# A gated attention + Fourier-mixing kernel: operands of the next sequence product at an even rate, reciprocals fifteen steps behind their load, x blocks a cycle sooner

## The chip, the cores and the metric

One core of a Trainium2 chip. The metric is device time in microseconds (us) of one execution, the median over repeated runs; lower is better.

## The reference, cut to what matters

```python
g = sigmoid((A_x * gate_w).sum(-1, keepdims=True))      # A_x: 1 x 2048 x 640
q, k, v = split(A_x @ wqkv)                             # 32 heads of 20
o = softmax(q @ k.T * 20 ** -0.5) @ v
a = o @ wo
hr, hi = B_x @ dft_hid_re.T, B_x @ dft_hid_im.T         # 640 x 640 each
b = dft_seq_re @ hr - dft_seq_im @ hi                   # 2048 x 2048 each
out = g * a + (1 - g) * b
```

All is float32. The output is 2048 x 640.

## The kernel before, in words

**Precision and products.** TensorE multiplies in a rounded float32 form. Each operand is therefore split into a rounded part and its remainder (`split`: a CAST, L130 on POOL, and a subtraction, L131), and a product is three matmuls. Both Fourier products are done on halves by a scheme with seven products in place of eight: `FEATURE` lists those along the hidden axis, `PRODUCTS` those along the sequence. Each names the sum or difference of one or two blocks that makes its left operand, its right operand, and the one or two targets it is added to.

**The stages.** First the projections, up to about 230 us (queries, keys, values; spilled to DRAM as `qk_scr`, `v_scr`). Then one long loop of 256 cycles, in which attention is interleaved with fill work. Last a tail that applies `wo` to the final rows.

**The cycle.** An attention unit is one head pair and half of the queries; there are 32 (`NU`), each of 32 steps, and a cycle is four steps. In a cycle TensorE does 8 score matmuls for the exponentials (L1071, "e" in the string `ORDER`), 8 score matmuls for the row maxima of a unit that comes 43 steps later (L191, "m"), a share of the fill matmuls ("F"), and at its end ("B", `burst`) the 16 value matmuls of two key tiles (L716, into `av`). ACT takes the exponentials (L1077), DVE reduces the maxima (L193). Score matmuls share five PSUM banks `ps`: one can start when ACT or DVE has read the bank's last contents.

**The fill.** For 56 cycles (`HID`) it is the hidden product (L500): seven features of 8 cycles. A feature has a left operand `lefts` (made of x blocks loaded from `in_xh` into stage tiles and summed and split on POOL: `load_left`, a list of functions of which one runs per cycle) and two right sets (`load_right`, tile `wb`, loaded in two halves from `w_scr`, each set for 4 cycles). The result is read by ACT and DVE into a `raw` tile (L509, L510), added to its targets on POOL (L513) and spilled to `a_scr`. Then come 168 cycles of the sequence product (L797): seven products of 8 tiles, each tile 3 cycles and 16 `dft_step`s. Its operands are `c` (a Fourier matrix, loaded from `in_cdft`, summed in L658 or, the first two, L677, and split into `part`; one for each 8 dft steps) and 16 `a` tiles per product (loaded from `a_scr` as `araw` by `load_a`, L686, summed in L691 and split). Results are added to earlier ones in `finish_y` (L895) and spilled. The `a` tiles of a product are made while the product before it runs. Last come 30 half tiles of the output projection.

**Who queues what.** Every engine takes its instructions in the order of the program. Nearly all transfers are issued by one queue, SP: an instruction there that waits (for data to be written, for a buffer to come free, or for an earlier transfer's landing) holds all transfers behind it. `at_step(i, fn)` puts a function's instructions at step i, whichever engines they go to.

**The end of a unit** (`unit_end`). ACT copies `av` to `o`; the row of sums goes to DRAM (`store_l`, L730) and comes back over 128 partitions (`load_l`, L733, tile `lc`); DVE takes the reciprocal (`recip`, L736); that goes out and comes back as a broadcast (`store_r`, L739, `load_r`, L743, tile `rb`); POOL multiplies (`norm`, L746); `store_o` (L754) writes `o_scr`. These seven stand at the steps in the tuple `steps`. The row maxima of a unit are turned in `turn_max`, whose result goes through DRAM too (L234, L240), in every unit.

**Calls that the change touches.** `run_extras` runs once a cycle: it issues at most one `load_a` and finishes at most one. `load_c_first` loads the first two `c` of the sequence product while the hidden stage still runs; the function that it returns does the POOL work.

Of the kernel before, what the change touches and what calls it, by code (L numbers as in the profile page):

```python
# [83 lines left out]
def f32(ap):  # L84
    return ap.bitcast(F32)
# [3 lines left out]
def mix_kernel(ctx: ExitStack, tc: tile.TileContext, xa, xh, wqk, wb, wr, cdft, wo, out):  # L89
# [61 lines left out]
    def raw_tile():  # L151
        return work.tile([P, 1024], F32, name="raw", bufs=3)
# [24 lines left out]
    def at_step(i, fn):  # L177
        later.setdefault(i, []).append(fn)
# [251 lines left out]
    def load_left(n, stage):  # L430
        terms = FEATURE[n][0]
        hi, lo = [block(z, 2 + n % 2) for z in range(2)]

        def load(q):
            c = slice(1024 * q, min(1024 * q + 1024, ND * 512))
            raws = stage(q)[:, : len(terms), : c.stop - c.start]
            at = sorted(2 * th + dh for _, th, dh in terms)
            sp.dma_start(raws, xh[at[0] : at[-1] + 1 : max(at[-1] - at[0], 1), :, c].rearrange("t p c -> p t c"))
            return raws

        def slab(j, raws):
            c = slice(512 * j, 512 * j + 512)
            parts = [raws[:, z, j % 2 * 512 : j % 2 * 512 + 512] for z in range(len(terms))]
            a = parts[0]
            if len(terms) > 1:
                one, two = parts if terms[0][1:] < terms[1][1:] else parts[::-1]
                pool.tensor_tensor(a, one, two, op=ALU.add if terms[1][0] > 0 else ALU.subtract)  # L447
            split(hi[:, c], lo[:, c], a, pool, pool)

        lefts[n] = [l.rearrange("p (d c) -> p d c", d=ND) for l in (hi, lo)]  # L450
        raws = {}

        def step_(j):
            def fn():
                if j < 2:
                    raws[j] = load(j)
                if j:
                    slab(j - 1, raws[(j - 1) // 2])
                if j == 2:
                    raws[2] = load(2)  # L460
            return fn

        return [step_(j) for j in range(ND + 1)]

    def own_stage(q):
        return f32(stages[q % 2])
# [193 lines left out]

        return finish

    c_raws = []

    def load_c_first(g):
        if g == 0:
            w = f32(wide.tile([P, 2, ND, BW], R, name="wb", bufs=2)).rearrange("p z d c -> p (z d c)")
            c_raws.extend(w[:, 1024 * q : 1024 * q + 1024] for q in range(3))
        (_, th, ri), (sign, th2, ri2) = PRODUCTS[0][0]
        raws = [c_raws.pop(0) if c_raws else raw_tile() for _ in range(2)]  # L670
        for raw, (half, part) in zip(raws, ((th, ri), (th2, ri2))):
            o = (2 * part + g % 2) * 1024
            sp.dma_start(raw, cdft[half * HT + g // 2, :, o : o + 1024])

        def finish():
            c = cparts[g] = part_tile()
            pool.tensor_tensor(raws[0], raws[0], raws[1], op=ALU.add if sign > 0 else ALU.subtract)  # L677
            split(c[:, 0], c[:, 1], raws[0], pool, pool)

        return finish  # L680
# [40 lines left out]
    def unit_end(i, n):  # L721
        o = pa.tile([P, 512], F32, name="o", bufs=2)
        act.activation(o, av, AF.Copy)
        lc = pa.tile([P, 16], F32, name="lc")
        rb = pa.tile([P, 512], F32, name="rb")

        q = pool if n == NU - 1 else sp

        def store_l():
            q.dma_start(l_scr[n], o.rearrange("(j r) c -> j r c", j=4)[:, DH])  # L730

        def load_l():
            q.dma_start(lc, l_scr[n].rearrange("j (a b) -> (j a) b", b=16))  # L733

        def recip():
            dve.reciprocal(lc, lc)  # L736

        def store_r():
            q.dma_start(r_scr[n].rearrange("j (a b) -> (j a) b", b=16), lc)  # L739

        def load_r():
            for j in range(4):
                q.dma_start(rb[32 * j : 32 * j + 32, :], r_scr[n, j : j + 1].to_broadcast([32, 512]))  # L743

        def norm():
            pool.tensor_tensor(o, o, rb, op=ALU.mult)  # L746

        def store_o():
            for qc in range(2):
                for h in range(2):  # L750
                    j = 2 * qc + h
                    t0 = (n % 2) * (S // 2) + qc * 512
                    r = (2 * (n // 2) + h) * DH
                    q.dma_start(o_scr[r : r + DH, t0 : t0 + 512], o[32 * j : 32 * j + DH, :])  # L754

        if n == NU - 1:
            chain.extend((o, rb))
            return
        steps = (6, 10, 18, 25, 29, 36, 46) if n < NU - 2 else (1, 4, 10, 12, 15, 19, 21)
        for k, fn in zip(steps, (store_l, load_l, recip, store_r, load_r, norm, store_o)):  # L760
            at_step(i + k, fn)

# [11 lines left out]
    def dft_step(g):  # L774
        n, t, s = g // NS // HT, g // NS % HT, g % NS
        if s == 0:
            new_y(0), new_y(1)
            outs[n, t] = []
        if s % 8 == 0 and g // 8 + 3 < 2 * UNITS:
            cfin.append(load_c(g // 8 + 3))  # L780
        if s % 8 == 4 and cfin and 2 < g // 8 + 2 < 2 * UNITS:
            cfin.pop(0)()
        if s == 8:
            for _, th, hf in PRODUCTS[n][2]:
                tt = th * HT + t
                y = None
                if (tt, hf) in signs:
                    y = apool[0].tile([P, HE], F32, name="yt", bufs=4)
                    sp.dma_start(y, y_scr[tt, :, hf * HE : (hf + 1) * HE])
                outs[n, t].append(y)  # L790
        c = cparts[g // 8]
        cs = slice((s % 8) * P, (s % 8 + 1) * P)
        a = at[n % 2, s]
        for z, (cz, az) in enumerate(((0, 0), (0, 1), (1, 0))):
            for h in range(2):
                r = slice(64 * h, 64 * h + 64)
                pe.matmul(yp[h][:, :HE], c[r, cz, cs], a[r, az], start=s == 0 and z == 0, stop=s == NS - 1 and z == 2)  # L797
            if z < 2:
                yield
        w = g % (HT * NS) - 16  # L800
        if n + 1 == len(PRODUCTS) and w >= 0:
            d, r = divmod(w, 8)
            if r == 0 and d < ND:
                wos[d] = raw_tile()[:, :D]
                sp.dma_start(wos[d], wo[:, d])
            if r == 5 and d < ND:
                raw = wos.pop(d)
                for h in range(2):
                    wos[d, h] = a_tile(1, 2 * d + h)
                    split(wos[d, h][:, 0], wos[d, h][:, 1], raw[:, h * HE : (h + 1) * HE], pool, pool)  # L810
        if s == NS - 1:
            m = apool[0].tile([P, HE], F32, name="m", bufs=2)
            y0, y1 = yp[0][:, :HE], yp[1][:, :HE]

            def read():
                act.activation(m, y0, AF.Copy)
                dve.tensor_tensor(m, y1, m, op=ALU.add)

            extras.append((now[0], read))
            for out_, y in zip(PRODUCTS[n][2], outs.pop((n, t))):  # L820
                extras.append((now[0] + 5, functools.partial(finish_y, out_, t, m, y)))
        yield
# [33 lines left out]
    def out_tile(tt, hf):  # L856
# [7 lines left out]
        for d in range(ND - 1):  # L864
            for z, (oz, wz) in enumerate(((0, 0), (0, 1), (1, 0))):
# [5 lines left out]
        m = apool[0].tile([P, HE], F32, name="m", bufs=2)  # L871
        y0, y1 = yp[0][:, :HE], yp[1][:, :HE]
        g = gate[:, tt : tt + 1]

# [33 lines left out]
    def run_extras(g, most):  # L908
        while extras and most and extras[0][0] <= now[0]:
            extras.pop(0)[1]()  # L910
            most -= 1
        if more(g):
            n = g // (HT * NS) + 1
            preps.append(load_a(n, made.setdefault(n, 0)))
            made[n] += 1
        if len(preps) > 2 or preps and not more(g):
            preps.pop(0)()

    def more(g):
        n, w = divmod(g, HT * NS)  # L920
        return n + 1 < len(PRODUCTS) and w >= 16 and made.get(n + 1, 0) < NS

    apool = []

# [93 lines left out]
    def end(i):  # L1018
        if i % 4 == 2:
            c = i // 4  # L1020
            n, k = divmod(c, 8)
            if c < HID:
                if c % 4 == 0 and 2 <= c // 4 + 1 < SETS:
                    for q, fn in enumerate(load_right(c // 4 + 1)):
                        at_step(i + 1 + 4 * q, fn)
                if k == 0 and n + 1 < len(FEATURE):
                    slabs.extend(load_left(n + 1, own_stage))
                if slabs:
# [5 lines left out]
                    at_step(i + 2, make_a_early)  # L1034
                if HID - 8 <= c < HID - 2:
                    at_step(i + 4, make_a_early)
                if c in (HID - 4, HID - 2):
                    at_step(i + 5, load_c_first((c - HID + 4) // 2))
            if c == HID:
                make_a_early()  # L1040
                make_a_early()
# [90 lines left out]
    def out_half(tt, hf, y, ops, add, shared=False):  # L1132
# [4 lines left out]
        ye = y[:, hf * HE : (hf + 1) * HE]  # L1137
        g = gate[:, tt : tt + 1]
        if shared:
            m = apool[0].tile([P, HE], F32, name="m", bufs=2)  # L1140
# [99 lines left out]
```

## Time and profile before

| | before |
|---|---|
| median of 3 runs | 1878.33 us (1878.31 to 1878.79) |
| the profiled execution's own time | 1871.42 us |
| its span | 1869.6 us |
| TensorE busy | 1844.7 us, 99% |
| DVE / POOL / ACT busy | 78% / 70% / 66% |

The profiled execution was 6.9 us shorter than the median of the runs without a profile; its span is the part of it between the first and the last instruction. TensorE's busy time is modelled at the ends of its matmuls, so 99% does not say that it works at its best rate. L numbers are lines of the kernel before; in the one after, lines behind the function `load_c_first` are lower by 4.

### The profile page before, as it was taken

How to read it: one execution, taken by the hardware profiler on the slowest of the kernel's cores; microseconds unless marked ns; L12 is line 12 of the kernel's file. 1: busy time of each engine (PE TensorE's matmuls, PEld its weight loads, DVE VectorE, ACT ScalarE, POOL GpSimd, SP SyncE). 2: the span in 40 equal slices, each digit the busy share in tenths (PEclk: the TensorE clock that was granted, in tenths of full speed). 3: DMA queues.
4: the chain of work that ended last, by engine and by line, in shares of the span. 5: the costliest groups of instructions: out<-in, count | busy, mean ns of one | idle time of the engine just before them, and what ended most of it. 6: DMA issues, size and time to landing. Idle time of an engine off the chain costs nothing. (4 is left out here: it accounts for less than half of the span.)

```text
span 1869.6 us, 45887 instructions
## 1 busy us (share of the span) xinstructions
PE 1844.7 (99%) x17917; PEld 1339.1 (72%) x17917; DVE 1459.2 (78%) x2428; ACT 1236.0 (66%) x2378; POOL 1300.1 (70%) x1098
## 2 busy tenths in 40 slices
PE   9999999999999999999999999899999999999998
PEld 8988876676676677776777767667777677766666
DVE  4157488888888888888888888788888888889953
ACT  4233377677676676676776767567767677677785
POOL 1379635566486998566799899868779988734344
PEclk9999999999999999999999999999999999999999
DMA  7887874887886774536577676546486756542214
GB/s 234 202 267 285 256 225 120 205 229 169 233 209 192 226 215 149 139 116 182 184 210 234 164 238 192 166 131 197 137 231 212 212 175 180 157 103 76 63 54 155
DMA packets 194445, 342.26 MB, mean 183 GB/s; under 512 B 53951, under 2 KB 107327, under 8 KB 193971
## 3 DMA queue, kind: packets, MB, share of 16 engines
q1 hardware_dynamic: 193267, 337.35, 61.7%
q0 software_dynamic: 960, 1.97, 0.6%
q8 instruction: 141, 2.31, 0.5%
q14 instruction: 77, 0.63, 0.1%
HBM read 257.79 MB, written 81.28 MB: 181 GB/s over the span
## 5 line engine op out<-in xcount | busy, mean ns | idle before, releaser
L193 DVE TENSOR_REDUCE mx<-ps 128x1 f32<-128x512 f32 x2048 | 1299.4, 685 | 211.4 <-PE ps L191 192.1
L1077 ACT ACTIVATE p<-ps 128x512 f32<-128x512 f32 x2048 | 1087.3, 598 | 440.0 <-PE ps L191 229.9
L191 PE MATMUL ps<-kst,qst 60*128 60x512 f32 x2048 | 778.7, 414 | 11.1 <-DVE mx L193 10.8
L1071 PE MATMUL ps<-qst,kst 62*128 62x512 f32 x2048 | 695.8, 414 | 0.0
L797 PE MATMUL yp<-x,part 64*128 64x320 f32 x5376 | 644.3, 306 | 0.0
L797 PEld LDWEIGHTS yp<-x,part 64*128 64x128 f32 x5376 | 582.3, 186 | 7.2
L716 PE MATMUL av<-p,v 128*21 128x512 f32 x4096 | 495.3, 599 | 0.0
L1071 PEld LDWEIGHTS ps<-qst,kst 62*128 62x128 f32 x2048 | 333.3, 185 | 223.0 <-DVE mx L193 131.5
L191 PEld LDWEIGHTS ps<-kst,qst 60*128 60x128 f32 x2048 | 368.2, 184 | 23.6 <-DVE mx L193 11.9
L131 POOL TENSOR_TENSOR part<-raw,part 128x1024 fp32r<-128x1024 f32 (+3 forms) x134 | 296.8, 2215 | 10.2
L716 PEld LDWEIGHTS av<-p,v 128*21 128x21 f32 x4096 | 95.6, 100 | 209.5 <-issue 208.5
L130 POOL CAST part<-raw 128x1024 fp32r<-128x1024 f32 (+2 forms) x127 | 125.0, 985 | 135.5 <-PE yp L797 102.3
L500 PE MATMUL yp<-wb,x 64*128 64x320 f32 x1680 | 209.3, 308 | 4.9 <-ACT raw L509 3.3
L658 POOL TENSOR_TENSOR raw<-raw,raw 128x1024 f32<-128x1024 f32 x78 | 188.1, 2412 | 33.2 <-DMA raw<-in_cdft 21.4
L500 PEld LDWEIGHTS yp<-wb,x 64*128 64x128 f32 x1680 | 180.8, 186 | 8.9 <-ACT raw L509 3.9
L131 POOL TENSOR_TENSOR x<-araw,x 128x320 fp32r<-128x320 f32 x96 | 83.8, 873 | 7.7
L868 PE MATMUL yp<-x,part 64*128 64x320 f32 x720 | 87.3, 309 | 0.0
L513 POOL TENSOR_TENSOR x<-x,raw 128x640 f32<-128x640 f32 x40 | 62.5, 1562 | 29.9 <-DVE raw L510 17.8
L885 POOL TENSOR_TENSOR x<-x,m 128x320 f32<-128x320 f32 x30 | 26.2, 873 | 81.9 <-DVE m L880 66.8
L868 PEld LDWEIGHTS yp<-x,part 64*128 64x128 f32 x720 | 75.4, 185 | 2.7
L691 POOL TENSOR_TENSOR araw<-araw 128x320 f32<-128x320 f32 x80 | 69.9, 874 | 2.9 <-DMA araw<-a_scr 2.9
L447 POOL TENSOR_TENSOR part<-part 128x512 f32<-128x512 f32 x25 | 32.3, 1292 | 46.1 <-PE ps L191 22.8
(107 smaller groups left out, 1394.3 us busy)
## 6 DMA issues: line engine op xcount, KB each, us to landing
raw<-in_cdft SPq DMA_DIRECT2D x189, 512.0 KB
araw<-a_scr SPq DMA_DIRECT2D x176, 160.0 KB
wb<-w_scr SPq DMA_DIRECT2D x28, 800.0 KB
qk_scr<-p SPq DMA_DIRECT2D x40, 512.0 KB
kst<-qk_scr SPq DMA_DIRECT2D x90, 160.0 KB
qst<-qk_scr SPq DMA_DIRECT2D x90, 160.0 KB
part<-in_xh SPq DMA_DIRECT2D x10, 1024.0 KB
yt<-y_scr SPq DMA_DIRECT2D x64, 160.0 KB
```

The lines of the kernel that those rows point to most:

```text
L130: e1.tensor_copy(dst1, src)
L131: e2.tensor_tensor(dst2, src, f32(dst1), op=ALU.subtract)
L191: pe.matmul(ps, q[b : b + KROWS, qt * P : (qt + 1) * P], k[b : b + KROWS, kc * 512 : (kc + 1) * 512], start=True, stop=True)
L193: return lambda: dve.tensor_reduce(mx[n][:, h, qt, kc : kc + 1], ps, axis=AX.X, op=ALU.max)
L500: pe.matmul(ps[z], lefts[n][a][r, d, k * P : k * P + P], rights[2 * n + hf][r, b, d], start=done_ == 0, stop=done_ == 3 * ND - 1)
L658: pool.tensor_tensor(raws[0], raws[0], raws[1], op=ALU.add if PRODUCTS[n][0][1][0] > 0 else ALU.subtract)
L691: pool.tensor_tensor(raws[0], raws[0], raws[1], op=ALU.add if PRODUCTS[n][1][1][0] > 0 else ALU.subtract)
L716: pe.matmul(av[32 * j : 32 * j + DH + 1, :], v[:, kt, h * (DH + 1) : (h + 1) * (DH + 1)], pp[qc][:, h, :], start=kt == 0, stop=kt == NS - 1)
L797: pe.matmul(yp[h][:, :HE], c[r, cz, cs], a[r, az], start=s == 0 and z == 0, stop=s == NS - 1 and z == 2)
L868: pe.matmul(yp[h][:, :HE], o[r, oz, d], wos[d, hf][r, wz], start=d == 0 and z == 0, stop=d == ND - 2 and z == 2)
L1071: pe.matmul(pt, k[b : b + KROWS + 2, kt * P : (kt + 1) * P], q[b : b + KROWS + 2, qc * 512 : (qc + 1) * 512], start=True, stop=True)
L1077: act.activation(pts[n, kt, qc][:, h], pt, AF.Exp, scale=float(DH) ** -0.5)
```

## The change

Six edits, in the same file:

- `load_left`: the sum and split of an x block run two steps of the list after its load, not one, so the list is one longer. The third load comes at the fourth entry, not the third.
- `load_right` calls: the second half of a set is issued 2 steps after the first, not 4.
- `load_c_first`: is called two cycles sooner, for c = HID - 6 and HID - 4; its POOL work stands 9 steps later, not 5. The first pair goes to the block that will hold `a` tiles 12 to 15, the second to the free `wb` tile.
- `unit_end`: new steps.
- the tile `m`: three buffers, not two (in all three places).
- `run_extras`: a `load_a` is issued when 7 more dft steps of the product have gone by (from the 11th on), not in every cycle from the 16th on, and its POOL work is due 8 steps after its load.

```diff
-                if j:
-                    slab(j - 1, raws[(j - 1) // 2])
-                if j == 2:
+                if j > 1:
+                    slab(j - 2, raws[(j - 2) // 2])
+                if j == 3:
                     raws[2] = load(2)
...
-        return [step_(j) for j in range(ND + 1)]
+        return [step_(j) for j in range(ND + 2)]
...
-    c_raws = []
-
     def load_c_first(g):
-        if g == 0:
-            w = f32(wide.tile([P, 2, ND, BW], R, name="wb", bufs=2)).rearrange("p z d c -> p (z d c)")
-            c_raws.extend(w[:, 1024 * q : 1024 * q + 1024] for q in range(3))
+        w = f32(wide.tile([P, 2, ND, BW], R, name="wb", bufs=2)).rearrange("p z d c -> p (z d c)") if g else f32(block(1, 3))
         (_, th, ri), (sign, th2, ri2) = PRODUCTS[0][0]
-        raws = [c_raws.pop(0) if c_raws else raw_tile() for _ in range(2)]
+        raws = [w[:, 1024 * q : 1024 * q + 1024] for q in range(2)]
...
-        steps = (6, 10, 18, 25, 29, 36, 46) if n < NU - 2 else (1, 4, 10, 12, 15, 19, 21)
+        steps = (4, 8, 23, 26, 30, 38, 47) if n < NU - 2 else (1, 4, 10, 12, 15, 19, 21)
         for k, fn in zip(steps, (store_l, load_l, recip, store_r, load_r, norm, store_o)):
             at_step(i + k, fn)
...
-            m = apool[0].tile([P, HE], F32, name="m", bufs=2)
+            m = apool[0].tile([P, HE], F32, name="m", bufs=3)
...
         if more(g):
             n = g // (HT * NS) + 1
-            preps.append(load_a(n, made.setdefault(n, 0)))
+            preps.append((now[0] + 8, load_a(n, made.setdefault(n, 0))))
             made[n] += 1
-        if len(preps) > 2 or preps and not more(g):
-            preps.pop(0)()
+        if preps and preps[0][0] <= now[0]:
+            preps.pop(0)[1]()

     def more(g):
         n, w = divmod(g, HT * NS)
-        return n + 1 < len(PRODUCTS) and w >= 16 and made.get(n + 1, 0) < NS
+        return n + 1 < len(PRODUCTS) and made.get(n + 1, 0) < min(NS, (w - 4) // 7)
...
-                        at_step(i + 1 + 4 * q, fn)
+                        at_step(i + 1 + 2 * q, fn)
...
-                if c in (HID - 4, HID - 2):
-                    at_step(i + 5, load_c_first((c - HID + 4) // 2))
+                if c in (HID - 6, HID - 4):
+                    at_step(i + 9, load_c_first((c - HID + 6) // 2))
```

On SP, in the hidden stage where the second right set of the fifth feature is loaded (`wb` twice: its two halves; `in_xh`: x blocks of the next feature; `kst`: keys of the next head pair), before:

```order
L438 DMA part<-in_xh 128x1024
L1006 DMA kst_92<-qk_scr 20x4x512
L1006 DMA wb<-w_scr 64x2x1600
L1006 DMA kst_92<-qk_scr 20x4x512 x2
L1006 DMA a_scr<-part 128x640
L560 DMA v<-v_scr 128x672
L1006 DMA kst_92<-qk_scr 20x4x512
L730 DMA l_scr<-o 4x512
L438 DMA part<-in_xh 128x1024
L1006 DMA kst_92<-qk_scr 20x4x512
L1006 DMA wb<-w_scr 64x2x1600
```

and now:

```order
L438 DMA part<-in_xh 128x1024
L1002 DMA kst_92<-qk_scr 20x4x512
L1002 DMA wb<-w_scr 64x2x1600
L1002 DMA kst_92<-qk_scr 20x4x512
L726 DMA l_scr<-o 4x512
L1002 DMA kst_92<-qk_scr 20x4x512
L1002 DMA wb<-w_scr 64x2x1600
L1002 DMA a_scr<-part 128x640
L560 DMA v<-v_scr 128x672
L1002 DMA kst_92<-qk_scr 20x4x512
L438 DMA part<-in_xh 128x1024
```

The second half of the set has moved ahead of five transfers, one of them the next x block; the store of the sums, `l_scr`, has moved up too and still stands before it.

On SP, some 20 steps later in the same unit, where the reciprocals go out (`r_scr`) and the turned maxima too (`m_scr`, and back into `qst`), before:

```order
L1006 DMA a_scr<-x_2662 128x640
L1006 DMA wb<-w_scr 64x2x1600
L739 DMA r_scr<-lc 128x16
L234 DMA m_scr<-m 128x64
L1006 DMA a_scr<-x_2662 128x640
L240 DMA qst_93<-m_scr 1x32x32 x4
L743 DMA rb<-r_scr 32x512 x4
```

and now:

```order
L1002 DMA wb<-w_scr 64x2x1600 x2
L1002 DMA a_scr<-x_2662 128x640
L234 DMA m_scr<-m 128x64
L735 DMA r_scr<-lc 128x16
L1002 DMA a_scr<-x_2662 128x640
L240 DMA qst_93<-m_scr 1x32x32 x4
L739 DMA rb<-r_scr 32x512 x4
```

The store of the reciprocals now stands behind that of the maxima.

On POOL, in the last cycles of the hidden stage (the pairs L130 and L131 with `x` make `a` tiles of the first sequence product, L513 adds hidden results, and the three with 128x1024 make the first `c`), before:

```order
L513 TENSOR_TENSOR x_3493<-x_3493,raw 128x640
L130 CAST x_8217<-part 128x320
L131 TENSOR_TENSOR x_8217<-part,x_8217 128x320
L677 TENSOR_TENSOR wb<-wb 128x1024
L130 CAST part<-wb 128x1024
L131 TENSOR_TENSOR part<-wb,part 128x1024
L130 CAST x_8217<-part 128x320
L131 TENSOR_TENSOR x_8217<-part,x_8217 128x320
L513 TENSOR_TENSOR x_3897<-x_3897,raw 128x640
```

and now:

```order
L673 TENSOR_TENSOR x_7960<-x_7960 128x1024
L130 CAST part<-x_7960 128x1024
L131 TENSOR_TENSOR part<-x_7960,part 128x1024
L130 CAST x_8223<-part 128x320
L131 TENSOR_TENSOR x_8223<-part,x_8223 128x320
L513 TENSOR_TENSOR x_3493<-x_3493,raw 128x640
L130 CAST x_8223<-part 128x320
L131 TENSOR_TENSOR x_8223<-part,x_8223 128x320
L130 CAST x_8223<-part 128x320
L131 TENSOR_TENSOR x_8223<-part,x_8223 128x320
L513 TENSOR_TENSOR x_3894<-x_3894,raw 128x640
```

The first `c` has moved ahead of one hidden result and two `a` tiles, about a cycle.

More of the change, by code (lines that the diff above doesn't have):

```diff
@@ L870, in out_tile @@
                     yield
-        m = apool[0].tile([P, HE], F32, name="m", bufs=2)
+        m = apool[0].tile([P, HE], F32, name="m", bufs=3)
         y0, y1 = yp[0][:, :HE], yp[1][:, :HE]
@@ L1139, in out_half @@
         if shared:
-            m = apool[0].tile([P, HE], F32, name="m", bufs=2)
+            m = apool[0].tile([P, HE], F32, name="m", bufs=3)
             act.activation(m, ps, AF.Copy, scale=g)
```

## The prediction

> **What bounds the kernel now.** I read the page's first part, then the spacing of TensorE's work over time, then its waits, then who made them last.
>
> ```profile
> PE 1844.7 (99%) x17917; PEld 1339.1 (72%) x17917; DVE 1459.2 (78%) x2428; ACT 1236.0 (66%) x2378; POOL 1300.1 (70%) x1098
> ```
>
> TensorE is the bound, and the change leaves its matmuls as they are. So only time that it loses can be won. The busy share hides part of that loss, since it can be busy at a lower clock. A better measure is the start of the 16 value matmuls that end each cycle (timeline of PE: start, length, line, count). Two quiet stretches give the normal cycle, five others are too long:
>
> ```profile
> 355.23 0.63 PE L716 MATMUL av<-p,v 128*21 128x512 f32 x4
> 372.30 0.63 PE L716 MATMUL av<-p,v 128*21 128x512 f32 x4
> 460.01 0.63 PE L716 MATMUL av<-p,v 128*21 128x512 f32 x4
> 478.58 1.06 PE L716 MATMUL av<-p,v 128*21 128x512 f32 x8
> 566.25 0.63 PE L716 MATMUL av<-p,v 128*21 128x512 f32 x4
> 573.57 0.63 PE L716 MATMUL av<-p,v 128*21 128x512 f32 x4
> 586.13 1.06 PE L716 MATMUL av<-p,v 128*21 128x512 f32 x8
> 595.40 1.06 PE L716 MATMUL av<-p,v 128*21 128x512 f32 x8
> 1176.08 0.63 PE L716 MATMUL av<-p,v 128*21 128x512 f32 x4
> 1196.40 1.06 PE L716 MATMUL av<-p,v 128*21 128x512 f32 x8
> 1675.95 1.06 PE L716 MATMUL av<-p,v 128*21 128x512 f32 x8
> ```
>
> Hidden stage: 14 cycles from 372.30 to 460.01, 6.265 us each. Sequence stage: 76 cycles from 1196.40 to 1675.95, 6.31 us each. Against these: A, two cycles from 355.23: 17.07 - 12.53 = 4.54 too long. B, two from 460.01: 18.57 - 12.53 = 6.04. C, one from 566.25: 7.32 - 6.265 = 1.05. D, one from 586.13: 9.27 - 6.265 = 3.00. E, two from 1176.08: 20.32 - 12.62 = 7.70. Together 22.3 us, 1.2% of the time, 14.6 of it in the hidden stage. Their causes, in the waits of TensorE and DVE (us in total, times, longest):
>
> ```profile
> PE ps L191 <- DVE mx L193: 10.8, 4, 5.9
> PE yp L500 <- ACT raw L509: 3.3, 2, 2.7
> PE yp L500 <- DMA wb<-w_scr: 1.6, 1, 1.6
> DVE lc L736 <- DMA lc<-l_scr: 12.2, 4, 6.1
> ```
>
> The four PE waits on the row maxima are DVE standing at the reciprocal, because `lc` has not landed; no bank of maxima comes free meanwhile. The timeline has all four, here with the issue of the first and the last load, and TensorE's wait behind the first:
>
> ```profile
> 346.70 0.35 SPq L733 DMA_DIRECT2D lc<-l_scr  x1
> 361.85 0.25 DVE L736 RECIPROCAL lc<-lc 128x16 f32<-128x16 f32 x1 [2.24 <-DMA lc<-l_scr]
> 362.70 0.50 PE L191 MATMUL ps<-kst,qst 60*128 60x512 f32 x1 [1.81 <-DVE mx L193]
> 468.25 0.25 DVE L736 RECIPROCAL lc<-lc 128x16 f32<-128x16 f32 x1 [2.75 <-DMA lc<-l_scr]
> 571.02 0.25 DVE L736 RECIPROCAL lc<-lc 128x16 f32<-128x16 f32 x1 [1.07 <-DMA lc<-l_scr]
> 1176.36 0.33 SPq L733 DMA_DIRECT2D lc<-l_scr  x1
> 1185.89 0.25 DVE L736 RECIPROCAL lc<-lc 128x16 f32<-128x16 f32 x1 [6.11 <-DMA lc<-l_scr]
> ```
>
> So A, B, C and E hold one each. In A stands another short one (the smaller of the two waits on `raw`, 3.3 - 2.7 = 0.6), in B the late `wb` half, and D is the other `raw` wait. The gaps sum to 10.8 + 3.3 + 1.6 = 15.7 us; the other 6.6 are slow matmuls behind them:
>
> ```profile
> 350.00:370.00 20.00, 17.64 (x159) 11.13 (x149) 13.65 (x25) 11.10 (x23) 14.07 (x12) 0.91 0.81 202
> 1180.00:1190.00 10.00, 4.13 (x33) 3.37 (x33) 3.67 (x7) 1.76 (x4) 9.65 (x11) 0.67 0.62 155
> 1200.00:1210.00 10.00, 10.00 (x110) 7.27 (x110) 8.71 (x15) 7.16 (x14) 4.45 (x3) 1.00 0.61 181
> ```
>
> In the first two of these stretches the granted clock (third number from the end) is 0.91 and 0.67; in the last, a quiet one, 1.00. In A the gaps are 0.6 + 1.81 = 2.4 of 4.54 us, so a short wait costs nearly its length again. The Trainium skill ("TensorE: Matmul & The Clock Gate", Part 1) has the clock halve only after an idle window of about 3.4 us; by that, only E would have slow matmuls behind it, and the loss to be won would be 15.7 + (7.70 - 5.9) = 17.5. The trace speaks against it in A.
>
> **The reciprocal.** It moves from step 18 to 23, its load from 10 to 8. A step is 6.27 / 4 = 1.57 us, so DVE comes to it 7.8 us later. Before, DVE came 2.24, 2.75, 1.07 and 6.11 too soon. Even if the loads land no sooner, 5.1 us are spare in the hidden stage and 1.7 in E; the two steps sooner in the queue (up to 3.1 us) come on top. The term is the 10.8 us of gaps with their slow matmuls: of A all but the 0.6, 3.9; of B by its share of the waits, 6.04 x 2.75 / (2.75 + 1.62) = 3.8; C 1.05; E 7.70; some 16.5.
>
> What it could cost: the store of the reciprocals now waits for an instruction 5 steps later, and holds all of SP behind it.
>
> ```profile
> SPq L234 <- DVE m L131: 208.9, 28, 10.7
> SPq L739 <- DVE lc L736: 104.4, 14, 20.6
> ```
>
> But SP already waits 208.9 / 28 = 7.5 us at the store of the turned maxima, for a DVE instruction in a burst behind the new place of the reciprocal. The reciprocals' store now stands behind that one, so it finds its data ready and adds nothing. I take 0; without this cover it would be up to 5 steps, 7.8 us, of late transfers in a unit. `norm` gets 8 steps behind `load_r`, before 7. The store of the sums stands 2 steps sooner, and SP can wait there 3.1 us longer for ACT; behind it stand `kst` loads with 8 steps to spare, and the second `wb` half.
>
> **Second half of a right set.**
>
> ```profile
> 436.96 0.64 SPq L1006 DMA_DIRECT2D wb<-w_scr  x1
> 450.92 0.64 SPq L1006 DMA_DIRECT2D wb<-w_scr  x1
> 464.12 0.38 PE L500 MATMUL yp<-wb,x 64*128 64x320 f32 x1 [1.62 <-DMA wb<-w_scr]
> ```
>
> It took 13.2 us to land and was 1.62 late. It stands 2 steps sooner, and ahead of the x block. That is 3.1 us at least, so the wait goes, worth the rest of B, 6.04 - 3.8 = 2.2. The x block behind it comes some us later, but its sum stands a whole cycle (6.27) later. I put x blocks and the third `m` buffer at 0: no PE wait names either.
>
> **First `c` operands.**
>
> ```profile
> 573.26 0.88 SPq L673 DMA_DIRECT2D wb<-in_cdft  x2
> 581.89 2.40 POOL L677 TENSOR_TENSOR wb<-wb 128x1024 f32<-128x1024 f32 x1 [10.87 <-PE av L716]
> 589.17 1.53 POOL L513 TENSOR_TENSOR x<-x,raw 128x640 f32<-128x640 f32 x1
> 590.73 0.44 ACT L509 ACTIVATE raw<-yp 128x320 f32<-128x320 f32 x1 [3.46 <-POOL x L513]
> ```
>
> POOL stood 10.87 us at the first sum (the releaser named is long done; it ends 8.6 us after the loads' issue), so the hidden result behind it was added late, `raw` stayed taken, and D followed. Now the loads are called two cycles (12.5 us) sooner and the sum only one. The loads have 9 steps (14.1 us), more than 8.6. D goes: 3.00. What is late next on POOL has 10.87 us more room.
>
> **Even rate of the `a` tiles.** On POOL, E's surroundings give the price of one `y` pair, one `a` tile (from its start to the next) and one `c` (sum to the next CAST):
>
> ```profile
> 1180.61 1.68 POOL L895 TENSOR_TENSOR yt<-yt,m 128x320 f32<-128x320 f32 x2
> 1182.24 0.87 POOL L691 TENSOR_TENSOR araw<-araw 128x320 f32<-128x320 f32 x1
> 1184.52 0.86 POOL L691 TENSOR_TENSOR araw<-araw 128x320 f32<-128x320 f32 x1
> 1186.79 2.37 POOL L658 TENSOR_TENSOR raw<-raw,raw 128x1024 f32<-128x1024 f32 x1
> 1192.65 1.06 POOL L130 CAST part<-raw 128x1024 fp32r<-128x1024 f32 x1
> ```
>
> An `a` tile is 2.28, a `c` 5.86. Where both have two terms, a cycle needs 16/24 x 5.86 = 3.91, plus 8/24 x 1.68 = 0.56, plus one `a`: 6.75 against a cycle of 6.31, for 16 cycles. Now it is 16 `a` tiles in some 22 cycles, 1.66: 6.13. POOL stops falling behind by 0.44 us a cycle. TensorE doesn't wait for it today, so I take 0; it helps SP, which waits for these buffers.
>
> **Sum.** 16.5 + 2.2 + 3.0 = 21.7, and the 0.6 in A: the 22.3 us, near enough. For that 0.6 the x block's third load now stands behind a store of `raw` that it stood ahead of. Removing waits exposes others, though: the transfers stay as dense as they are. I leave one new wait of the mean size of the old four, 10.8 / 4 = 2.7. So 19.6 us go: the profiled execution from 1871.42 to 1851.8, the median (6.9 us above it) from 1878.33 to 1858.7.
>
> **Rivals.**
>
> *The waits move (0.20).* In the hidden stage SP is held by transfers' landings, a load of 8 KB took 15.15 us, and sooner transfers only change who is late. For it: A to D hold waits of three kinds. Against it: each late one gets 3 us or more. E goes and half of the hidden stage's loss stays: 1878.33 - 7.70 - 7.3 = 1863.3; with all of it, 1870.6.
>
> *The slow matmuls stay (0.08).* Of the 6.6 us of slow matmuls, 7.70 - 5.9 = 1.8 follow the one long wait. The other 4.8 could have a cause that isn't the short waits ahead of them, and stay: 1858.7 + 4.8 = 1863.5. For it speaks only that the waits and the clock are read from one execution; against it, that the clock is 1.00 in the quiet stretch. By the 3.4 us of the Trainium skill's page above it would be so.
>
> *POOL comes too late for a product's first tile (0.08), slower.* The last `a` tile is now made at the product's end, about 16 dft steps (3 cycles, 18.9 us) ahead of its use; before, by its place in the code, some 6 cycles. POOL was busy 9.65 of 10 us around E. If its lag passes 18.9 us, TensorE waits at each of six product starts. At the price of E, that is 6 x 7.70 = 46.2, less 22.3: 1902. Against it: 6.13 is under 6.31, so the lag shouldn't grow.
>
> *It does nothing (0.04).* The DMA could land later than 15 steps, or fresh waits use the whole gain: 1878.
>
> **Numbers.** The forecast, 1858.7, has 0.60. Low end: all 22.3 go (1856.0), and a part of the 6.9 us that the runs have over the profile is waits of the same kind: 1851. High end: only E goes, 1871. Outside are the slower case, the case of no change and a little more. A measurement tells 0.2%, 3.8 us, from none. Faster by more: 0.60 + 0.20 + 0.08 = 0.88; same 0.04; slower 0.08.
>
> **What would show it.** DVE's waits for `lc` and PE's waits on `mx` behind them are gone, and 1180 to 1190 has no counterpart at a clock of 0.67. No wait on `wb<-w_scr`; POOL's first sum of `c` waits under 2 us. SP's wait at the reciprocals' store shrinks from 104.4, and its wait at the turned maxima doesn't grow by more than that. All cycles of the sequence stage near 6.31. I am wrong if PE waits for `part`, `x` or `wb` that it didn't wait for before, or if the 22.3 us go and the median doesn't follow.

## The result, and the profile after

| | before | after |
|---|---|---|
| median | 1878.32 us (1874.48 to 1878.79) | 1862.75 us (1861.49 to 1863.75) |
| profiled execution, span | 1871.42, 1869.6 us | 1862.77, 1861.0 us |

The kernel got faster: ratio 0.9921, with an interval of 0.9904 to 0.9938. That is 15.6 us; 19.6 were forecast, and 1862.75 lies in the range but next to the rival "the waits move" (1863.3). On a second chip the same pair had 0.9951 (0.9933 to 0.9969), 9.2 us. Before's median there was 1873.05 us over 29 runs, and 1873.95 and 1873.63 on the two other chips used below, so its four runs in the table are some 5 us higher than elsewhere; whether the chip or the draw made them so is not known.

The page's first part shows the same work, TensorE still the bound:

```profile
PE 1843.7 (99%) x17917; PEld 1343.2 (72%) x17917; DVE 1459.7 (78%) x2428; ACT 1236.9 (66%) x2378; POOL 1300.6 (70%) x1098
```

The spacing of the value matmuls after (timeline of PE), at the places where before lost its time:

```profile
461.31 0.63 PE L712 MATMUL av<-p,v 128*21 128x512 f32 x4
472.90 0.63 PE L712 MATMUL av<-p,v 128*21 128x512 f32 x4
567.11 0.63 PE L712 MATMUL av<-p,v 128*21 128x512 f32 x4
581.02 0.63 PE L712 MATMUL av<-p,v 128*21 128x512 f32 x4
1174.93 0.63 PE L712 MATMUL av<-p,v 128*21 128x512 f32 x4
1187.54 0.63 PE L712 MATMUL av<-p,v 128*21 128x512 f32 x4
```

The last two rows bound two cycles: 12.61 us, against 20.32 in E. E is gone. But the first pair bounds one cycle of the hidden stage, 11.59 us long, and the second pair one of 13.91: 5.33 and 7.64 too long. They stand where B and C were. Summed over all cycles, with 6.265 us for a normal one of the hidden stage and 6.31 in the sequence stage, before lost 14.8 us in the hidden stage and 8.0 in the sequence stage; after loses 14.1 and 1.2. (These sums take in small losses too, so they are a little above the 14.6 and 7.70 of the prediction.) Of the 8.6 us between the two spans, 0.7 come from the hidden stage.

What took the old waits' place stands in the waits of TensorE, and in the timeline of PE with the two waits:

```profile
PE ps L191 <- DMA qst<-qk_scr: 4.8, 1, 4.8
PE ps L191 <- DMA o_scr<-o: 3.8, 2, 3.5
467.10 0.76 PE L191 MATMUL ps<-kst,qst 60*128 60x512 f32 x1 [3.45 <-DMA o_scr<-o]
574.30 0.76 PE L191 MATMUL ps<-kst,qst 60*128 60x512 f32 x1 [4.85 <-DMA qst<-qk_scr]
```

No wait on `mx`, `wb` or `raw` is left. Both new ones are at L191, the first row-maximum matmul of a head pair, which needs that pair's keys and queries. The first row names a store as releaser, but L191 doesn't read that; SP's timeline shows the last query loads just ahead:

```profile
456.33 4.26 SPq L1002 DMA_DIRECT2D qst<-qk_scr  x4
462.37 3.02 SPq L750 DMA_DIRECT2D o_scr<-o  x4
```

The fourth was issued by 460.6 and TensorE went on at 467.10, at least 6.5 us later. I take its landing for what ended the wait. The same two places before:

```profile
461.30 4.21 SPq L1006 DMA_DIRECT2D qst<-qk_scr  x3
474.19 0.50 PE L191 MATMUL ps<-kst,qst 60*128 60x512 f32 x1
```

There the last one was issued by 465.5, and TensorE, held up in B by other waits, came 8.7 us later and found it landed. The old waits had covered the queries.

### The profile page after: what moved, and what is told of

It is laid out like the page before. It is cut to its first block, busy times and chain, and to the rows that moved or that the text cites. A ratio compares the mean times of both kernels' runs of the same rounds, so it can differ in the third digit from the quotient of the medians.

```text
span 1861.0 us, 45882 instructions
## 1 busy us (share of the span) xinstructions
PE 1843.7 (99%) x17917; PEld 1343.2 (72%) x17917; DVE 1459.7 (78%) x2428; ACT 1236.9 (66%) x2378; POOL 1300.6 (70%) x1098
## 5 line engine op out<-in xcount | busy, mean ns | idle before, releaser
L191 PE MATMUL ps<-kst,qst 60*128 60x512 f32 x2048 | 777.3, 414 | 9.4 <-DMA qst<-qk_scr 4.8
L191 PEld LDWEIGHTS ps<-kst,qst 60*128 60x128 f32 x2048 | 368.4, 185 | 21.4 <-issue 8.9
L131 POOL TENSOR_TENSOR part<-raw,part 128x1024 fp32r<-128x1024 f32 (+3 forms) x134 | 296.7, 2214 | 10.2
L130 POOL CAST part<-raw 128x1024 fp32r<-128x1024 f32 (+2 forms) x127 | 125.0, 984 | 132.0 <-PE yp L793 96.0
L131 POOL TENSOR_TENSOR x<-araw,x 128x320 fp32r<-128x320 f32 x96 | 83.9, 874 | 7.7
L513 POOL TENSOR_TENSOR x<-x,raw 128x640 f32<-128x640 f32 x40 | 62.5, 1562 | 35.6 <-DVE raw L510 29.4
L363 PE MATMUL yp<-x,part 64*128 64x512 f32 x480 | 62.4, 390 | 0.0
```

The lines of the kernel that those rows point to most:

```text
L130: e1.tensor_copy(dst1, src)
L131: e2.tensor_tensor(dst2, src, f32(dst1), op=ALU.subtract)
L191: pe.matmul(ps, q[b : b + KROWS, qt * P : (qt + 1) * P], k[b : b + KROWS, kc * 512 : (kc + 1) * 512], start=True, stop=True)
```

## The experiments

**The stretch is full** is one account. Three stretches of the hidden stage, near 355, 460 and 570 us, hold more transfers than the DMA can move in time: the twelve key and query loads of a head pair, two halves of a right set, x blocks, spilled sums or the first `c`, all through SP. Some transfer is always last; take its wait away and the next one stops TensorE. (A queue held by instructions that wait for POOL would look much the same; the run with fewer bytes says more of that.) **Each wait for itself** is the other: every wait has its own cause, and an edit removes it for good.

For each run: median, ratio to before on the same chip (before had 1873.95, 1873.05 and 1873.63 on the three chips used), and the cycles' loss in its profile, hidden stage / sequence stage.

**Before, profiled once more** (no edit).

> The kernel before, unchanged, with a second profile. Its runs without a profile took 1878.3 us and its profiled one 1871.4, while the changed kernel took the same 1862.8 with and without. If the stalls of the kernel before differ from run to run, this profile shows about 1878 and 7 us more of waits of the five kinds A to E (most likely a longer wait for lc or for the query loads), beside the same quiet cycles. If the 6.9 us lie outside the span, this profile shows a span near 1870 again and a time near 1878.

1870.61 us, ratio 0.9990 (0.9970 to 1.0009), runs from 1864.8 to 1880.7; profiled execution 1880.72, loss 25.4 / 7.6.

```profile
PE yp L500 <- DMA wb<-w_scr: 12.7, 2, 7.7
PE ps L191 <- DVE mx L193: 7.8, 4, 4.3
PE yp L500 <- ACT raw L509: 2.3, 2, 1.2
```

Same kernel (the chip is another), same three places, another order of blame: in this execution the right sets cost most, in the first the reciprocals. The first profile was a light one. So part of the 6.9 us between that profile and the median is probably loss of this kind, and the hidden stage's loss is not a set of fixed waits.

**The new steps alone**, on before:

```diff
-        steps = (6, 10, 18, 25, 29, 36, 46) if n < NU - 2 else (1, 4, 10, 12, 15, 19, 21)
+        steps = (4, 8, 23, 26, 30, 38, 47) if n < NU - 2 else (1, 4, 10, 12, 15, 19, 21)
```

> The kernel before with the new steps of unit_end alone. My theory: the reciprocal waited for lc at eight steps, and no longer does at fifteen, so DVE's 12.2 us of waits and E (7.7 us) go; the hidden stage keeps D (3.0) and the late right set, and the last query load becomes the late one there: 1864 to 1871. Rival, that the even rate of the a tiles took E away (POOL held SP, and SP the load of lc): little goes with the steps alone, 1874 or more, and an lc wait of several us is left in the sequence stage.

1872.82 us, 0.9993 (0.9979 to 1.0006): no change that can be told, where a gain had been expected. Loss 21.3 / 3.4. The waits on `lc` and E are gone, as said, but:

```profile
PE yp L500 <- DMA wb<-w_scr: 6.8, 2, 5.6
PE yp L500 <- ACT raw L509: 4.7, 2, 3.4
```

The largest term of the prediction, taken by itself, was handed on to the right sets and the hidden results in the same stretches.

**After with the old steps** (the same line the other way round).

> The changed kernel with the old steps of unit_end. My theory: DVE waits for lc again, in two or more units by 1 to 6 us each: 1867 to 1876. Rival (the even rate and the other order of loads took the lc waits away): 1864 or less, and no lc wait over 1 us.

1865.77 us, 0.9949 (0.9932 to 0.9966), loss 17.7 / 0.9.

```profile
PE ps L191 <- DVE mx L193: 11.9, 3, 6.5
359.86 0.25 DVE L732 RECIPROCAL lc<-lc 128x16 f32<-128x16 f32 x1 [1.45 <-DMA lc<-l_scr]
467.52 0.25 DVE L732 RECIPROCAL lc<-lc 128x16 f32<-128x16 f32 x1 [6.71 <-DMA lc<-l_scr]
573.51 0.25 DVE L732 RECIPROCAL lc<-lc 128x16 f32<-128x16 f32 x1 [4.54 <-DMA lc<-l_scr]
```

The reciprocals wait again, 12.7 us in all, and all three of these waits lie in the three stretches; none is left in the sequence stage, so E doesn't come back with the old steps. The ratio is near those of after (0.9921 and 0.9951, on other chips): that the new steps bring anything on top of the other edits can't be told, and the waits on the queries, covered here, come in place of these. The waits came back as expected; the time is just under the 1867 to 1876 given.

**After with queries and keys loaded earlier**, two per step:

```diff
-                    at_step(i + 2 + j, functools.partial(sp.dma_start, *args))
+                    at_step(i + 2 + j // 2, functools.partial(sp.dma_start, *args))
```

> The changed kernel with the twelve loads of keys and queries of the next head pair at two a step, so the last of them stands 6 steps sooner and ahead of the second half of the right set, the second x block and the first c. My theory: the changed kernel's three waits of TensorE on the first row-maximum matmul of a head pair (4.85, 3.45 and 0.35 us, some 13.7 with the slow cycles behind them) are the last query load landing late; they go and the time is 1849 to 1854. Rival: the transfers of the hidden stage are simply too dense, and another of them becomes the late one (right set, x block, lc): 1859 or more.

1881.2 us, 1.0038 (1.0023 to 1.0053): slower than before. Loss 25.3 / 8.7.

```profile
PE yp L500 <- ACT raw L509: 10.1, 1, 10.1
PE yp L500 <- DMA wb<-w_scr: 7.9, 1, 7.9
PE ps L191 <- DMA o_scr<-o: 1.1, 1, 1.1
```

The wait on the queries is nearly gone, and what is behind them in the queue pays more than they did: ahead of the wait on `raw`, ACT stood 10.8 us at L509 until a spilled result (`a_scr<-raw`) had landed, and POOL 12.4 us for an x block issued at 347.94. By "each wait for itself" 9 to 14 us below after were to be won; that account falls here, and the full stretch is left.

**After, profiled once more** (no edit).

> The changed kernel, unchanged, on the chip of the three below, with a second profile. Theory now: in the hidden stage the loads of a head pair, the right sets, the x blocks and the spilled sums fill the transfers in three stretches (near 355, 460 and 570), and whichever lands last there stops TensorE; the changed order makes that 14 us in place of 15 to 25. So again 5 us or more near 460 and near 570, possibly behind another transfer, and no stall in the sequence stage: 1861 to 1865, before some 9 to 13 more. Rival (the query loads are the late ones, whatever else): the same two waits on the same loads.

1863.87 us, 0.9951 (0.9933 to 0.9969), loss 17.1 / 1.3.

```profile
PE ps L191 <- DMA o_scr<-o: 11.1, 2, 7.0
```

Two waits at the same two places, 4.09 and 6.97 us here. That TensorE waits for the queries is a property of the kernel after; its size is not.

**The even rate alone**, on before (the `run_extras` part of the diff and nothing else).

> The kernel before with the even rate of the a tiles alone. Theory: POOL's lag, and through the buffers SP's, made the lc load late in the sequence stage; at an even rate E (7.5 us) goes though the steps are the old ones, and the hidden stage is as before: 6 to 8 us under before. Rival (it takes the new steps): the sequence stage still has an lc wait of 3 us or more, and the time is within 3 us of before.

1870.69 us, 0.9986 (0.9965 to 1.0007), loss 16.5 / 1.5. E is gone here too, with the old steps, as the theory has it; but the time is only 2.4 us under before, not 6 to 8, so of what E cost in the profile little shows in the median.

```profile
PE ps L191 <- DVE mx L193: 4.4, 3, 2.3
PE yp L500 <- ACT raw L509: 4.3, 2, 2.8
PE yp L500 <- DMA wb<-w_scr: 1.3, 2, 0.9
```

**All but the steps and the even rate** (after, with `steps` and `run_extras` of before).

> The kernel before with the four edits of the hidden stage (x blocks, second half of a right set, first c, and the third m buffer), old steps, old rate. Theory: no wait on a right set and none on raw, lc waits near 460 and 570 in their place, E still there: hidden stage 17 to 18 us too long, as with the old steps above, so 0 to 6 us under before. Rival (these edits bring most of the gain): 8 us or more under before.

1868.69 us, 0.9976 (0.9955 to 0.9998), loss 14.8 / 6.9. E is back, here with a wait of 3.01 us (timeline of PE):

```profile
1184.26 0.79 PE L191 MATMUL ps<-kst,qst 60*128 60x512 f32 x1 [3.01 <-DVE mx L193]
```

So E goes with the steps alone or with the rate alone, and stays without both. By themselves steps, rate and the rest bring 0.07, 0.14 and 0.24%, together 0.45%; the whole brought 0.49% on the chip of the last two. Each of these has an interval of 0.13 to 0.22% to either side, and the first two include none at all, so that they add up isn't shown.

**Transfers taken out of the stretches**: after, with the values' load 24 steps later, the second x block one entry (a cycle) later, the first `c` loaded 4 steps later, behind the query loads, and summed 2 steps later.

```diff
-                if j < 2:
-                    raws[j] = load(j)
+                if j in (0, 2):
+                    raws[j // 2] = load(j // 2)
...
-                at_step(i + 6, functools.partial(load_v, p + 1))
+                at_step(i + 30, functools.partial(load_v, p + 1))
...
-                    at_step(i + 9, load_c_first((c - HID + 6) // 2))
+                    def c_first(i=i, g=(c - HID + 6) // 2):
+                        at_step(i + 11, load_c_first(g))
+                    at_step(i + 4, c_first)
```

> The changed kernel with three loads taken out of the dense stretches: the values of the next head pair at step 30, not 6; the second x block a cycle later; the first two c loads 4 steps later, behind the query loads, with their POOL work 2 steps later. Theory (density): the waits near 460 and 570 shrink by the time of what was moved ahead of the query loads, 336 KB to 1 MB each at some 200 GB/s, 2 to 5 us each: 1853 to 1858, no new wait. Rival (moving loads only changes which is late): 1861 or more, with a wait on an x block, raw or the first part.

1858.0 us, 0.9922 (0.9893 to 0.9950), loss 9.2 / 1.9; after on the same chip had 1863.87, 0.9951; the intervals overlap a little. The two waits on the queries shrink from 4.09 and 6.97 to 1.9 and 3.4.

**After with fewer bytes**: the loads of the second copies of the repeated parts left out. Its scores are not the right ones; it shows only what the transfers do to the time.

```diff
+                    if p > 1 and k == (2 if t is kst[p % 2] else 1):
+                        yield None
+                        continue
...
-                    at_step(i + 2 + j, functools.partial(sp.dma_start, *args))
+                    if args:
+                        at_step(i + 2 + j, functools.partial(sp.dma_start, *args))
```

> The changed kernel without four of the twelve loads of each later head pair: a head's keys and queries stand three times in the stacked operand, one part of them twice, and the second copy isn't loaded (the old pair's stays there, so the scores are another's). All other loads keep their steps. It takes 640 KB out of each dense stretch, one of them ahead of the last query load. Theory (density: the last query load lands late because of what stands ahead of it): the waits near 461 and 569 of the changed kernel, 11.1 us in its second profile, fall by 2 to 4 us each, and with the slow cycles behind them the time is 5 to 10 us under the changed kernel's 1863. Rival (SP is held by POOL's or TensorE's work, not by transfers): within 3 us of it.

1852.88 us, 0.9888 (0.9870 to 0.9906), loss 7.2 / 2.1: by the ratios 0.6% under after, some 12 us, a little more than expected, so it matters how many bytes are moved, and a held queue is not the whole account. Near 460 no wait is left; near 563 the wait on the queries stays (windows: PE busy, PEld, DVE, ACT and POOL, then clock, the mean busy share of the 16 DMA engines and GB/s; first after, then this kernel):

```profile
435.00:480.00 45.00, 41.55 (x404) 29.65 (x404) 35.71 (x63) 29.24 (x58) 22.83 (x19) 0.96 0.87 210
540.00:590.00 50.00, 45.15 (x428) 32.11 (x427) 37.78 (x66) 30.96 (x62) 37.07 (x38) 0.93 0.80 211
```

```profile
435.00:480.00 45.00, 45.00 (x456) 31.78 (x456) 40.20 (x70) 32.59 (x65) 24.48 (x20) 1.00 0.80 196
540.00:590.00 50.00, 44.98 (x434) 32.02 (x432) 38.11 (x66) 31.85 (x64) 39.32 (x41) 0.93 0.72 183
```

In the first stretch the DMA share is 0.80 against 0.87, and TensorE never stops. In the second it is 0.72, and a wait of 5.0 us is left; but this mean hides the part that counts: from 545 to 568 us, while the last queries are on their way, the share is 0.95, against 0.94 in after (and 0.87 in the last kernel below). Nor does such a share decide by itself: from 445 to 467 us it is 0.88 here without a wait, and 0.83 in after with one. Among what stands ahead of those queries are the first `c`, which the next run moves away, and a load of spilled sums (L698), at which SP stood 5.6 us for POOL, with all transfers behind it held. So in this stretch a held queue is a rival to the full DMA. The last kernel, where that load stands behind the queries, has no such wait, but it moves other transfers too: these runs don't part the two.

**After with the old `load_c_first` and its old calls.**

> The changed kernel with the first c operands loaded as before. Theory: D is back (raw stays taken near 590, 1.5 to 3 us and more with slow cycles), and the wait near 570 shrinks, since the 1 MB no longer stands ahead of the last three query loads: from 7 to 9 us too long to 3 to 6. So the two nearly cancel: within 4 us of the changed kernel. Rival (the move is what brought the gain): 5 us or more over it.

1862.86 us, 0.9934 (0.9914 to 0.9954), loss 15.0 / 1.2. The mechanism expected failed twice: D did not come back (that cycle is 0.39 too long), and the loss near 570 didn't shrink (7.86, with a wait of 4.76). That edit alone neither removed D nor made the new wait near 570; of the runs here only the last one clears that place, with x blocks and spilled sums moved too.

**After with the right set's second half 4 steps behind again.**

```diff
-                        at_step(i + 1 + 2 * q, fn)
+                        at_step(i + 1 + 4 * q, fn)
```

> The changed kernel with the second half of a right set issued 4 steps after the first, as before. Theory: the half stands behind the x block again and TensorE waits for it near 460, by 1 to 7 us as in the profiles of before, in place of the wait for the query loads: 0 to 6 us over the changed kernel. Rival (nothing but the sum of the transfers counts, whichever is last): within 2 us of it.

1867.6 us, 0.9964 (0.9944 to 0.9984), loss 20.2 / 1.6.

```profile
PE yp L500 <- DMA wb<-w_scr: 9.1, 2, 5.7
PE ps L191 <- DMA qst<-qk_scr: 1.9, 1, 1.9
PE ps L191 <- DMA a_scr<-raw: 1.8, 1, 1.8
```

The wait on `wb` comes back, and the queries' waits are smaller. It is 4.7 us slower than the kernel above it on the same chip, and 0.9964 against 0.9951 for after on another; the intervals overlap, so that it costs something is likely, and how much is not settled.

**More taken out of the stretches**: the spread kernel, and besides the first x block of a feature is loaded a cycle sooner (the list starts a cycle sooner and is one longer, so the other loads keep their cycles and stand one entry later), and one load of four spilled sums stands 7 steps later. Against the spread kernel:

```diff
-                if j in (0, 2):
-                    raws[j // 2] = load(j // 2)
-                if j > 1:
-                    slab(j - 2, raws[(j - 2) // 2])
-                if j == 3:
-                    raws[2] = load(2)
+                if j == 0:
+                    raws[0] = load(0)
+                if j in (2, 3):
+                    slab(j - 2, raws[0])
+                if j in (3, 4):
+                    raws[j - 2] = load(j - 2)
+                if j > 4:
+                    slab(j - 3, raws[(j - 3) // 2])
...
-        return [step_(j) for j in range(ND + 2)]
+        return [step_(j) for j in range(ND + 3)]
...
-                if k == 0 and n + 1 < len(FEATURE):
-                    slabs.extend(load_left(n + 1, own_stage))
+                if c == 0:
+                    slabs.extend(load_left(1, own_stage))
+                    slabs.pop(0)()
+                if k == 7 and n + 2 < len(FEATURE):
+                    slabs.extend(load_left(n + 2, own_stage))
...
-                        load_a_early(s, s + 4)
+                        if s == 4:
+                            at_step(i + 7, functools.partial(load_a_early, s, s + 4))
+                        else:
+                            load_a_early(s, s + 4)
```

> The spread version (1858.0) with two more loads taken out of the dense stretches: the first x block of a feature is loaded in the last cycle of the feature before, the others a cycle later than there, and one load of four spilled sums for the first sequence product stands 7 steps later, behind the query loads. Theory (density): the waits left near 461 (1.9 us) and 567 (3.4 us), 9 us with their slow cycles, mostly go: 1850 to 1855. Rival: the first x block meets the stage tile still in use, SP is held, and the time is 1858 or more.

1854.98 us, 0.9894 (0.9877 to 0.9911), the best kernel that computes everything. Loss 0.0 / 4.4: nothing is lost in the hidden stage (windows as above).

```profile
435.00:480.00 45.00, 45.00 (x459) 32.38 (x458) 40.17 (x70) 33.09 (x66) 24.49 (x20) 1.00 0.78 191
540.00:590.00 50.00, 50.00 (x510) 35.39 (x506) 44.10 (x75) 36.73 (x72) 39.14 (x40) 1.00 0.76 203
```

The bytes are the same, and most transfers stand where they did; all three stretches run without a stop. Its runs lie within 4.2 us of one another (1852.94 to 1857.14), those of before on that chip within 16. Of its 4.4 us in the sequence stage, 2.7 are one cycle at 601 where the first product's split operands are late.

## Why the prediction was right or wrong

**Direction and range** held, and so did "faster" with its reason: only TensorE's lost time could be won. The size did not come about as worked out, and that the median is near the forecast is in part luck: the profiled execution was to fall by 19.6 us, to 1851.8, and fell by 8.6, to 1862.77. The forecast then added before's 6.9 us between profile and median, which after doesn't have, so two errors partly cancel. On the second chip the median fell by 9.2 us, where 19.6 were forecast.

**E, 7.70 us: right in size, incomplete in cause.** 1180 to 1190 after:

```profile
1180.00:1190.00 10.00, 10.00 (x109) 6.42 (x108) 8.68 (x17) 6.26 (x13) 9.71 (x9) 1.00 0.69 223
```

Clock 1.00, no gap. The 7.70 us were given to the steps, and the even rate was put at 0 since "TensorE doesn't wait for it today". By its own argument that it helps SP it should have shared the term: the rate alone removes E as well.

**A to D, 14.6 less one new wait of 2.7: the step that failed.** Between the two profiles 0.7 us of it went. The waits on `lc`, `wb` and `raw` did go, as worked out; but in their place came two waits on the queries, 3.45 and 4.85 us, whose cycles lost 5.33 and 7.64: 13.0 us where 2.7 had been set. The step took the mean of the old waits for the new one, and counted one. It should have asked, for each stretch, which transfer lands next to last and how much later TensorE would have come to need it; the queries in B had no slack once the cover was gone. Steps alone with no gain, then queries early with a loss, then a stretch without loss when its transfers are spread, show that the wait moves; how much of the queries' lateness is a full DMA and how much a held queue stays open near 570. The rival "the waits move" had the mechanism. Its 1863.3 took half of the hidden stage's loss as won; between the profiles nearly all of it stayed, so that this number fits is the same luck.

**That the median still fell by 15.6 us** comes, as far as is known, from the other side of the subtraction, the runs of before. Before's second profile lost 25.4 us in the hidden stage, its first 14.8; after's two lost 14.1 and 17.1. How much the hidden stage won on the mean can't be had from two profiles each.

**Second half of the right set, 2.2 us: right in kind.** (B's 6.04 us were divided by a wait of DVE, 2.75, and one of TensorE, 1.62; by TensorE's own two waits, 2.32 and 1.62, this share is 2.5. The sum stays.) No wait on `wb` after; with the old place 9.1 us of them, and a time some us longer.

**First `c`, D 3.0 us: gone, but not as said.** POOL was to wait under 2 us at the first sum:

```profile
560.80 2.45 SPq L669 DMA_DIRECT2D x<-in_cdft  x2
571.43 2.34 POOL L673 TENSOR_TENSOR x<-x 128x1024 f32<-128x1024 f32 x1 [8.81 <-DMA x<-in_cdft]
```

It waited 8.81. POOL came at 562.62, 1.8 us after the first load's issue: nine steps in the program are not nine steps on SP, which ran that far behind. The landing itself took 8.2 to 10.6 us, near the 8.6 taken. What removed D instead isn't settled: with the old `load_c_first` it stayed away. The x blocks' edit, which moves POOL's work, wasn't tried alone, nor was the third `m` buffer.

**SP's stores: nearly right.** The wait at the reciprocals' store fell from 104.4 us to 4.4, that at the maxima's rose by 114.6, 10 more than the bound given:

```profile
SPq L234 <- DVE m L131: 323.5, 29, 30.3
SPq L735 <- DVE lc L732: 4.4, 1, 4.4
```

**Slow matmuls stay: no.** They come and go with the waits (below). But "a short wait costs nearly its length again" is too general: of the 6.6 us, 2.2 lie in A, 2.1 in B and 1.8 in E, and only 0.2 and 0.3 in C and D. **POOL too late for a first tile: no.** The last `a` tile of a product was ready 14.3 to 21.0 us before its first use, and the sequence stage lost 1.2 us in all.

## What to carry to other kernels

Where many transfers meet in one queue, a wait on one of them is not a price that can be struck off: find the stretch, list its transfers by the time they land and by the time they are needed, and price the second latest before taking away the latest. Here, moving transfers ahead in a full stretch moved the wait to their neighbours, and moving enough of them out of the stretch took it away. Look also for an instruction at which the queue itself is held. The kernel whose runs differ by 1% lost its time in such places, and one profile showed only one draw of it.

## What the runs showed of the hardware

The clock falls after some short waits and not after others. Matmuls that start after a wait, and the windows behind them (windows and timeline of PE; first the spread kernel, then the one spread more, then after, then before at D):

```profile
465.49 0.47 PE L191 MATMUL ps<-kst,qst 60*128 60x512 f32 x1 [1.93 <-DMA o_scr<-o]
466.00:470.00 4.00, 4.00 (x32) 4.00 (x30) 2.83 (x5) 2.21 (x4) 3.92 (x4) 0.57 0.92 223
```

```profile
606.23 0.70 PE L795 MATMUL yp<-x,part 64*128 64x320 f32 x6 [1.64 <-POOL part L131]
606.20:610.20 4.00, 3.97 (x44) 3.46 (x48) 2.92 (x5) 2.25 (x5) 3.86 (x3) 1.00 0.92 289
```

```profile
574.00:580.00 6.00, 5.70 (x38) 5.73 (x40) 3.08 (x6) 2.80 (x5) 5.84 (x5) 0.53 0.97 334
```

```profile
591.22 0.47 PE L500 MATMUL yp<-wb,x 64*128 64x320 f32 x2 [2.74 <-ACT raw L509]
590.00:610.00 20.00, 18.78 (x190) 13.43 (x192) 16.24 (x26) 14.01 (x27) 19.25 (x22) 1.00 0.49 156
```

After 1.93 us the granted clock was 0.57 over the next 4 us; after 4.85 it was 0.53 over 6 us; after 1.64, and after 2.74 in D, it stayed at 1.00. So the length alone doesn't decide. The clock records show what does. Between 240 and 1800 us every fall is to 0.50, and it lasts 3.41 us or two or three times that. Within an execution the falls begin whole multiples of 3.413 us apart: in before at 364.29, 470.11 and 1183.49 us, 31 and 209 of them.

Cut each profile into windows of this length, such that falls begin at their edges. In all the 13 profiles that have falls, a window at full clock in which TensorE, by the modelled ends of its matmuls, stood idle for 1.81 us or more was followed by one at half clock, and one with 1.65 us or less was not. The 1.81 us in A lay within one window; the 2.74 us in D lay across two, with 1.09 and 1.65.

What a wait costs therefore depends on where it falls. The cycle with 1.93 lost 3.86 us and those after with 3.45 and 4.85 lost 5.33 and 7.64, so each of these waits cost 1.9 to 2.8 us on top of its length. D's 2.74 cost 0.3 on top, and the wait of 1.64 with one of 0.56 ahead of it 0.5. The Trainium skill ("TensorE: Matmul & The Clock Gate", Part 1) has the clock halve after an idle window of about 3.4 us; these runs agree on the half clock and on the length of the window, but TensorE needn't be idle through all of it.
